# An S5 recurrence beside a gated MLP: output base made with the layer norm, B u over runs of 512 tokens, another order of first loads, another cut of the last tile

## The chip, the cores and the metric

One core of one Trainium2 chip. The metric is device time in microseconds of one launch, as a median of several executions. The span of a profile, from first to last instruction, is about 2 us shorter than the time of the same execution. The kernel before takes 274.86 us (274.7 to 275.23, 4 runs).

## The reference, cut to what matters

```python
xn = _layernorm(x)                      # x: 1 x 2048 x 640
# A: Bu = xn B_bar^T; h = Lam_bar * h + Bu, token by token; y = 2 Re(h C^T) + xn * Dskip
# B: z = gelu(xn w_in); z2 = layernorm(second half of z);
#    g = w_sp z2 + b_sp (mixes over all tokens); (z1 * g) w_out
return x + A(xn) + B(xn)
```

The term `x + xn * Dskip` needs no matmul. It is called *base* below.

## The kernel before

The program is a list of operations with reads, writes and rough durations. A list scheduler inside the kernel puts each engine's operations in an order by a model of their times; TensorE's order is as written. The chip then runs each engine's queue in that order. Token tiles are counted from 0: T0, T1, T2 are the transposes of the first three, x0, x1, x2 the loads of their input. LN is the layer norm. An eviction is the copy of a finished matmul result out of PSUM. The stages are: LN of 16 tiles, the transposes and z2; B u; z1; the mixing over tokens ("spatial products", by a Strassen-like scheme of seven products); the output tiles. VectorE runs the recurrence (`horner`, `scan`) beside them, and ScalarE afterwards adds the state that comes from earlier chunks (`fix`).

The parts that the change touches:

```python
FIRST = "x0 x1 h002 h025 x2 x3 h102 h125 x4 x5"   # loads; h002: half 0 of w_in, k tiles 0 and 1 (h105: half 1, k tiles 0 to 4)
...
def xn_T(i, b=None):                   # transposes of tile i on PE, one copy out of PSUM
    pe(tr, [xn.iv(), ident_m.iv()], [bank(b)], 0.3, "T%d" % i)
    act(lambda e: e.copy(xnTv[:, :, i * 128:(i + 1) * 128], v), ...)
...
def bu(q, jg, half):                   # 4 of every 8 tokens of a half
    rhs = [xnTv[:, k, half * 1024:(half + 1) * 1024].rearrange("p (m j) -> p m j", j=8)[:, :, jg * 4:jg * 4 + 4]
           for k in range(ND)]
...
def out_tile(j, half, b, last=False):
    dma("sp", bsm.ap(D), rows(A_x), ...)                                     # x again
    dve(... tensor_scalar(om, bsm, mean, rstd, subtract, mult) ...)          # xn again
    dve(... tensor_tensor(om, om, dk, mult) ...)                             # * Dskip
    dve(... tensor_tensor(om, om, bsm, add) ...)                             # + x
    ...  # 34 matmuls, each tile as two banks of 320 columns, alternating
    dve(... tensor_tensor(om, ps, om, add) ...)                              # last tile: 320 and 320
```

## Time and profile before

| stretch of the chain | from, us | length, us |
|---|---|---|
| head, to T2, the transposes of the third tile | 0 | 9.67 |
| z2 | 9.67 | 30.02 |
| B u, 200 matmuls | 39.69 | 45.00 |
| z1 | 84.70 | 29.20 |
| spatial products, 448 matmuls | 113.90 | 81.76 |
| output tiles | 195.66 | 73.96 |
| tail, to the end of the span | 269.62 | 3.1 |

The table is read from the chain of work that ended last. Its lines, with start, length and what ran:

```profile
9.67 0.45 PE ps L540 x5
...
39.69 45.00 PE ps L655 x200
...
113.90 81.76 PE ps L963 x448
195.66 2.72 PE ps L1053 x20
...
269.65 0.49 DVE arena L1076
270.14 0.40 DVEq L228
```

From 9.67 to 269.62 us the chain is TensorE alone, each piece starting where the last ends. So what other engines do in between costs nothing, as long as TensorE finds its operands. A B u matmul takes 45.00 / 200 = 225 ns; a spatial product of 432 columns takes 81.76 / 448 = 182.5 ns.

The head in the timeline (start, length, engine, line, operation; in brackets the idle time before it and what ended it):

```profile
5.50 0.98 DVE L526 TENSOR_SCALAR arena<-arena 128x640 bf16<-128x640 bf16 x2 [0.30 <-POOL arena L521]
6.01 0.98 PE L540 MATMUL ps<-arena 128*128 128x128 bf16 x10
6.70 0.49 DVE L515 BATCH_NORM_STATS2 arena<-arena 128x6 f32<-128x320 bf16 x1 [0.22 <-DMA arena<-in_A_x_dram]
7.47 2.00 PE L592 MATMUL ps<-arena 128*128 128x432 bf16 x10 [0.48 <-ACT arena L544]
9.67 0.45 PE L540 MATMUL ps<-arena 128*128 128x128 bf16 x5 [0.20 <-DVE arena L526]
```

L526 gives xn (the normalized x) of tiles 0 and 1, L540 at 6.01 is T0 and T1, L515 at 6.70 is the first statistic of x2, the moment x2 has landed. T2 is at 9.67.

The table of stretches for B u, spatial products and output (length; busy us of PE, PEld, DVE, ACT, POOL with counts; clock; DMA share; GB/s):

```profile
39.69:84.70 45.01, 45.01 (x202) 19.25 (x200) 37.16 (x86) 39.50 (x66) 3.52 (x4) 1.00 0.27 47
113.90:195.66 81.76, 81.76 (x450) 43.86 (x449) 78.11 (x164) 46.03 (x77) 0.00 (x0) 1.00 0.88 185
195.66:269.62 73.96, 73.95 (x544) 52.93 (x542) 50.34 (x115) 30.12 (x50) 0.00 (x0) 1.00 0.37 104
```

VectorE is busy for 50.34 of 73.96 us in the output stage; it has more room there than in the spatial products.

### The profile page before, as it was taken

To read this page: it belongs to the slowest core of one execution; us is meant where nothing else is said; L and a number is where in the kernel's file an instruction comes from. 1 tells how busy PE (TensorE), PEld (TensorE's weight loads), DVE (VectorE), ACT (ScalarE), POOL (GpSimd) and SP (SyncE) were. 2 spreads that over 40 slices of the span, in tenths; PEclk is the share of its full clock that TensorE was granted. 3 is DMA by queue.
4 is the path that set the end of the run, shared out by engine and by line. 5 is a ranking of instruction groups with operands and counts; after the bars stand their busy time and mean duration, and the time that the engine had idled before them with its cause. 6 is when DMAs were issued, how large, how long until landed. Compare 5 with 4: busy or idle time off the path is not lost.

```text
span 272.7 us, 4381 instructions
## 1 busy us (share of the span) xinstructions
PE 267.6 (98%) x1574; PEld 159.3 (58%) x1574; DVE 226.1 (83%) x551; ACT 164.7 (60%) x288; POOL 25.6 (9%) x54
## 2 busy tenths in 40 slices
PE   8999999999999999999999999999999999999995
PEld 3455554444446777755555555555577777777773
DVE  4988947588999999989999996999999995555442
ACT  2899999979976454523223228999999991000000
POOL 4445662200000000000000000000000000000000
PEclk9999999999999999999999999999999999999999
DMA  7999799400002974497996798699454645331201
GB/s 220 284 211 151 174 185 189 66 24 4 0 0 48 199 214 146 150 192 128 209 217 142 168 184 168 123 226 259 165 142 127 164 109 150 93 99 48 92 30 48
DMA packets 84883, 37.82 MB, mean 139 GB/s; under 512 B 70046, under 2 KB 84862, under 8 KB 84862
## 3 DMA queue, kind: packets, MB, share of 16 engines
q1 hardware_dynamic: 84718, 37.47, 61.4%
q8 instruction: 12, 0.20, 0.3%
q10 hardware_dynamic: 144, 0.08, 0.1%
q14 instruction: 9, 0.07, 0.1%
HBM read 12.29 MB, written 8.93 MB: 78 GB/s over the span
## 4 chain that ended last, share of the span: by engine, by line
PE 95%; DMA 1%; DVE 1%; SPq 1%; POOL 0%; issue 0%; DVEq 0%
PE ps L963 30%; PE ps L571 19%; PE ps L655 17%; PE ps L1053 16%; PE ps L1061 11%; PE ps L592 2%; DMA arena<-in_A_x_dram 1%; PE ps L540 1%; SPq L356 1%; DVE arena L515 0%; DVE arena L516 0%; POOL arena L521 0%; DVE arena L1076 0%; DVE arena L526 0%; DVEq L228 0%
## 5 line engine op out<-in xcount | busy, mean ns | idle before, releaser
L963 PE MATMUL ps<-arena 128*128 128x432 bf16 x448 | 81.9, 346 | 0.0
L963 PEld LDWEIGHTS ps<-arena 128*128 128x128 bf16 x448 | 43.8, 98 | 37.9
L571 PE MATMUL ps<-arena 128*128 128x432 bf16 x280 | 52.1, 346 | 0.0
L1053 PE MATMUL ps<-arena 128*128 128x320 bf16 x320 | 46.1, 299 | 0.0
L756 ACT ACTIVATE arena<-arena 128x512 bf16<-128x512 bf16 x70 | 44.0, 714 | 2.1 <-DVE arena L728 2.1
L655 PE MATMUL ps<-arena 128*128 128x512 bf16 x200 | 45.2, 386 | 0.0
L571 PEld LDWEIGHTS ps<-arena 128*128 128x128 bf16 x280 | 34.5, 124 | 15.6
L1053 PEld LDWEIGHTS ps<-arena 128*128 128x128 bf16 x320 | 31.2, 98 | 12.4
L976 ACT ACTIVATE arena<-ps,arena 128x432 f32<-128x432 f32 (+1 forms) x32 | 19.7, 615 | 29.4 <-PE ps L963 23.8
L655 PEld LDWEIGHTS ps<-arena 128*128 128x128 bf16 x200 | 19.2, 96 | 25.8
L1061 PE MATMUL ps<-arena 128*128 128x320 bf16 (+1 forms) x224 | 33.1, 299 | 0.0
L1061 PEld LDWEIGHTS ps<-arena 128*128 128x128 bf16 (+1 forms) x224 | 21.9, 98 | 8.5
L759 DVE TENSOR_TENSOR arena<-arena 128x512 bf16<-128x512 bf16 x70 | 26.2, 419 | 0.3 <-ACT arena L756 0.2
L686 DVE SCALAR_TENSOR_TENSOR arena<-arena 128x512 f32<-128x512 bf16 x35 | 25.8, 749 | 0.0
L662 ACT CAST arena<-ps 128x512 bf16<-128x512 f32 x40 | 21.3, 596 | 5.5 <-PE ps L655 5.4
L1070 DVE TENSOR_TENSOR arena<-ps,arena 128x640 bf16<-128x640 f32 x15 | 12.3, 823 | 12.7 <-PE ps L1061 12.6
L640 ACT ACTIVATE arena<-ps 128x864 bf16<-128x864 f32 x16 | 14.2, 890 | 13.5 <-PE ps L571 12.7
L920 DVE TENSOR_TENSOR arena<-arena 128x1024 bf16<-128x1024 bf16 x32 | 21.3, 686 | 1.2 <-PE ps L963 1.1
L708 DVE TENSOR_TENSOR arena<-arena 128x512 f32<-128x512 f32 (+2 forms) x40 | 21.6, 556 | 0.0
L691 DVE SCALAR_TENSOR_TENSOR arena<-arena 128x256 bf16<-128x256 bf16 (+1 forms) x35 | 16.8, 483 | 0.0
L688 DVE SCALAR_TENSOR_TENSOR arena<-arena 128x256 bf16<-128x256 bf16 (+1 forms) x35 | 16.7, 481 | 0.0
L1037 DVE TENSOR_SCALAR arena<-arena 128x640 bf16<-128x640 bf16 x16 | 7.1, 441 | 7.7 <-DMA out_dram<-arena 7.7
(99 smaller groups left out, 244.0 us busy)
## 6 DMA issues: line engine op xcount, KB each, us to landing
arena<-in_A_x_dram SPq DMA_DIRECT2D x32, 160.0 KB, 2.6
z_scratch<-arena SPq DMA_DIRECT2D x16, 216.0 KB, 2.2
arena<-z_scratch SPq DMA_DIRECT2D x8, 432.0 KB, 5.0
g_scratch<-arena SPq DMA_DIRECT2D x12, 224.0 KB, 2.9
out_dram<-arena SPq DMA_DIRECT2D x15, 160.0 KB, 2.2
arena<-in_B_w_in_dram SPq DMA_DIRECT2D x7, 216.0 KB, 3.6
arena<-in_B_w_out_dram SPq DMA_DIRECT2D x1, 960.0 KB, 6.7
arena<-in_B_w_in_dram SPq DMA_DIRECT2D x2, 324.0 KB, 4.3
```

Source lines behind the costliest of these rows:

```text
L571: r = e.matmul(ps[:, b + h, 0:FG], lhs(k), winv[:, k, hcol * FH + h * FG:hcol * FH + (h + 1) * FG], start=(k == 0), stop=(k == ND - 1))
L655: r = e.matmul(ps[:, b + ri, :], btv[:, ri, k, q * 128:(q + 1) * 128], rhs[k], start=(k == 0), stop=(k == ND - 1))
L662: act(lambda e, ri=ri: e.copy(o[:, ri, :, half, :], ps[:, b + ri, :].rearrange("p (m j) -> p j m", j=4)), [bank(b + ri)], [l_iv(q, jg * 4 ...
L686: dve(lambda e: e.scalar_tensor_tensor(tv, prev, lr, cur, op0=ALU.mult, op1=ALU.add), pr + [l_iv(q, j)] + cr, [t.iv()], cd(512) + PTR, nm ...
L708: tt = lambda o, a, b, op: (lambda e: e.tensor_tensor(o, a, b, op))
L756: act(lambda e, pv=pv, hv=hv, lo=lo, sc=sc: e.activation(pv, hv[:, lo:lo + 2, 1:257], ACT.Identity, scale=sc), [h.iv(), Civ(cn)], [m.iv()] ...
L759: dve(lambda e, m=m, lq=lq: e.tensor_tensor(lq, lq, m.ap(512), ALU.add), li + [m.iv()], li, cd(512, 2), "fix%s%d%d" % (nm, q, j))
L920: dve(lambda e: e.tensor_tensor(o.ap(1024), x.ap(1024), y.ap(1024), op), [x.iv(), y.iv()], [o.iv()], cd(1024, 2), "%s_%d" % (name, j))
L963: r = e.matmul(ps[:, bk, 0:FG], lv_[:, k, :], rv[k], start=(first and k == 0), stop=(k == 7), skip_group_check=True)
L976: act(lambda e: e.activation(o, pb(bk), ACT.Identity, bias=bias), [bank(bk)] + bi, [dst], ca(FG, psum=True, ptr=1), name)
L1053: r = e.matmul(ps[:, b + n, 0:320], hv[:, o:o + 128], cpv[:, ri, q, n * 320:(n + 1) * 320], start=(q == 0 and ri == 0), stop=False, skip_g ...
L1061: r = e.matmul(ps[:, b + n, 0:320], gv[0:kk, k, :], wov[0:kk, k, n * 320:(n + 1) * 320], start=False, stop=(k == 6), skip_group_check=True)
```

## The change

Its intent: compute base once, while x and xn are in SBUF, and spare the output stage its recomputation; read B u's moving operand in a row; let x2 come earlier and release the first z2 sooner; leave less to do after the last matmul. The list scheduler's model is altered too (its constants of latency and DMA rate, how it books transposing DMAs, and a rule for the first 12 us), and a fourth LN tile goes to ScalarE. The core of the diff, cut:

```diff
-    DMA_BW = 230e3
-    DMA_BW_T = 190e3
+    DMA_BW = 280e3
+    DMA_BW_T = 215e3
 ...
-            return g.add("dve", f, r, w, occ, 0.17, name, bias=bias)
+            return g.add("dve", f, r, w, occ, 0.13, name, bias=bias)
 ...                                          # act 0.2 -> 0.15, pool 0.15 -> 0.09
-        FIRST = "x0 x1 h002 h025 x2 x3 h102 h125 x4 x5"
+        FIRST = "x0 x1 h002 x2 h025 x3 h105 x4 x5"
-        ACT_LN = (6, 9, 12)
+        ACT_LN = (6, 8, 10, 12)
 ...
+            if i == 0:                        # T0 in two banks, copied out by two engines
+                act(lambda e: e.copy(xnTv[:, 0:3, 0:128], v[:, 0:3]), ...)
+                dve(lambda e: e.tensor_copy(xnTv[:, 3:5, 0:128], v2[:, 3:5]), ...)
 ...
+        def base(i):
+            dve(... tensor_tensor(m, xn, dk, mult) ...)
+            dve(... tensor_tensor(m, m, x, add) ...)
+            dma("sp", base_d[i * 128:(i + 1) * 128, :], m.ap(D), ...)
 ...
-        def bu(q, jg, half):
+        def bu(q, tq):
-            rhs = [... .rearrange("p (m j) -> p m j", j=8)[:, :, jg * 4:jg * 4 + 4] ...]
+                                     xnTv[:, k, tq * 512:(tq + 1) * 512], ...
 ...
-            dma("sp", bsm.ap(D), rows(A_x), ...)
-            ... xn, * Dskip, + x ...
+            dma("sp", bsm.ap(D), base_d.rearrange("(h r j) d -> h j r d", h=2, j=8)[half, j], ...)
 ...
+            cols = ((0, LASTN), (LASTN, D)) if last else ((0, 320), (320, D))    # LASTN = 480
```

In the last tile the 17 matmuls of the first 480 columns now all come before the 17 of the last 160.

More of the change, by code (lines that the diff above doesn't have):

```diff
@@ L29 @@
 class _Graph:
+    EPS0 = 0.12
+    TEPS = 12.0
     DMA_LAT = 2.0
-    DMA_BW = 230e3
-    DMA_BW_T = 190e3
+    DMA_BW = 280e3
+    DMA_BW_T = 215e3
     def __init__(self):
@@ L129, in schedule @@
                     s0 = min(max(f, o.rdy) for o in lst)
-                    cand = max((o for o in lst if max(f, o.rdy) <= s0 + eps), key=lambda o: o.tail)
+                    cand = max((o for o in lst if max(f, o.rdy) <= s0 + (self.EPS0 if s0 < self.TEPS else eps)), key=lambda o: o.tail)
                     st = max(f, cand.rdy)
@@ L141, in schedule @@
             if op.nbytes:
-                b0 = max(st + op.occ + 0.9, dma_free)
-                bw = self.DMA_BW_T if op.lat > 2.2 else self.DMA_BW
-                dma_free = b0 + op.nbytes / bw
-                op.done = dma_free + op.lat - 0.9
                 if op.lat > 2.2:
-                    free[eng] = max(free[eng], dma_free - 1.0)
+                    dma_free = max(st + 0.3, dma_free) + op.nbytes / self.DMA_BW_T
+                    free[eng] = max(free[eng], dma_free)
+                    op.done = max(st + op.occ, dma_free) + 1.7
+                else:
+                    dma_free = max(st + op.occ + 0.9, dma_free) + op.nbytes / self.DMA_BW
+                    op.done = dma_free + op.lat - 0.9
             else:
@@ L237, in bass_parallel_sum__ssm_conv_s5__mixer_gmlp__prompt_kernel @@
         g_d = nc.dram_tensor("g_scratch", [NT, 128, 896], BF16).ap()
-        stat_d = nc.dram_tensor("stat_scratch", [S, 2], FP32).ap()
+        base_d = nc.dram_tensor("base_scratch", [S, D], BF16).ap()
         class Mem:
@@ L287, in bass_parallel_sum__ssm_conv_s5__mixer_gmlp__prompt_kernel @@
         dk_m = top.sub(1280)
+        e4 = Mem(l_m.lo + 8192, 15 * 1280)
+        x_m += [e4.sub(1280) for _ in range(5)]
+        xn_m += [e4.sub(1280) for _ in range(10)]
+        base_m = [Mem(t_m[(1, 0, 2)[i // 5]].lo + i % 5 * 1280, 1280) for i in range(15)] + [Mem(l_m.lo + 38400, 1280)]
         hs_m = [top.sub(1548) for _ in range(5)]
@@ L335, in dve @@
         def dve(f, r, w, occ, name, bias=0.0):
-            return g.add("dve", f, r, w, occ, 0.17, name, bias=bias)
+            return g.add("dve", f, r, w, occ, 0.13, name, bias=bias)
         def act(f, r, w, occ, name, bias=0.0):
-            return g.add("act", f, r, w, occ, 0.2, name, bias=bias)
+            return g.add("act", f, r, w, occ, 0.15, name, bias=bias)
         def pool(f, r, w, occ, name, bias=0.0):
-            return g.add("pool", f, r, w, occ, 0.15, name, bias=bias)
+            return g.add("pool", f, r, w, occ, 0.09, name, bias=bias)
         def pe(f, r, w, occ, name):
@@ L408, in load_x @@
         def load_x(i, q="sp", bias=0.0):
-            m = x_m[i % 11]
+            m = x_m[i]
             xs[i] = m
@@ L488, in siv @@
             return st_m.iv((i * 16 + a) * 4, (b - a) * 4)
-        ACT_LN = (6, 9, 12)
+        ACT_LN = (6, 8, 10, 12)
         ACT_Z2 = (8, 12)
         NHALF = 4
+        LASTN = 480
         DMA_T = (10, 11, 12, 13, 14, 15)
@@ L501, in ln_x @@
             if i in ACT_LN:
-                sq = xn_m[i % 6]
+                sq = xn_m[i]
                 act(lambda e: e.activation(sq.ap(D), x, ACT.Copy, accum_out=stv[:, i, 0:1]),
@@ L522, in ln_x @@
                  [siv(i, 14, 15), Civ("half")], [ri], 0.5, "rstd%d" % i)
-            xn = xn_m[i % 6]
+            xn = xn_m[i]
             xns[i] = xn
@@ L536, in xn_T @@
             v = ps[:, b, :].bitcast(BF16)[:, 0:D].rearrange("p (u t) -> p u t", u=ND)
+            v2 = ps[:, 6, :].bitcast(BF16)[:, 0:D].rearrange("p (u t) -> p u t", u=ND)
             def tr(e):
                 for u in range(ND):
-                    r = e.transpose(v[:, u, :], xn.ap(D)[:, u * 128:(u + 1) * 128], ident_m.ap(128))
+                    r = e.transpose((v2 if i == 0 and u > 2 else v)[:, u, :], xn.ap(D)[:, u * 128:(u + 1) * 128], ident_m.ap(128))
                 return r
-            pe(tr, [xn.iv(), ident_m.iv()], [bank(b)], 0.3, "T%d" % i)
-            if i % 2 == 0 or i == 1:
+            pe(tr, [xn.iv(), ident_m.iv()], [bank(b)] + ([bank(6)] if i == 0 else []), 0.3, "T%d" % i)
+            if i == 0:
+                act(lambda e: e.copy(xnTv[:, 0:3, 0:128], v[:, 0:3]), [bank(b)],
+                    [xnT_m.iv(k * S * 2, 256) for k in range(3)], ca(384, psum=True), "xnT0a")
+                dve(lambda e: e.tensor_copy(xnTv[:, 3:5, 0:128], v2[:, 3:5]), [bank(6)],
+                    [xnT_m.iv(k * S * 2, 256) for k in (3, 4)], 0.21, "xnT0b")
+            elif i % 2 == 0 or i == 1:
                 act(lambda e: e.copy(xnTv[:, :, i * 128:(i + 1) * 128], v), [bank(b)], xnT_iv(i, i + 1),
@@ L547, in xn_T @@
                 dve(lambda e: e.tensor_copy(xnTv[:, :, i * 128:(i + 1) * 128], v), [bank(b)], xnT_iv(i, i + 1),
-                    cd(D), "xnT%d" % i)
-        def stats_turn():
-            for i in range(NT):
-                if i not in ACT_LN:
-                    pool(lambda e, i=i: e.tensor_copy(mrv[:, i, 0:1], stv[:, i, 12:13]), [siv(i, 12, 13)],
-                         [mr_m.iv(i * 8, 4)], 0.2, "mean%d" % i)
-            dma("sp", stat_d.rearrange("(t p) s -> p t s", p=128), mrv, [mr_m.iv()], [("statd", 0, 1)], 16384, "stst")
-            dma("sp", msv.rearrange("p (h j) s -> p h j s", h=2), stat_d.rearrange("(h r j) s -> r h j s", h=2, j=8),
-                [("statd", 0, 1)], [ms_m.iv()], 16384, "stld")
+                    0.41, "xnT%d" % i)
+        def base(i):
+            m, xn, xm = base_m[i], xns[i], xs[i]
+            dve(lambda e: e.tensor_tensor(m.ap(D), xn.ap(D), dk_m.ap(D), ALU.mult), [xn.iv(), dk_m.iv()], [m.iv()],
+                cd(D, 2), "xd%d" % i)
+            dve(lambda e: e.tensor_tensor(m.ap(D), m.ap(D), xm.ap(D), ALU.add), [m.iv(), xm.iv()], [m.iv()],
+                cd(D, 2), "base%d" % i)
+            dma("sp", base_d[i * 128:(i + 1) * 128, :], m.ap(D), [m.iv()], [("based", i, i + 1)], 128 * D * 2,
+                "bst%d" % i)
         st2v = st2_m.ap(NT * 8, FP32).rearrange("p (s t) -> p s t", t=NT)
@@ L593, in z2_half @@
                                            start=(k == 0), stop=(k == ND - 1)),
-                   xnT_iv(i, i + 1) + [win_m.iv((k * 2 * FH + c) * 2, FG * 2)], [bank(b)], 0.1825, "z2_%d%d.%d" % (i, h, k))
+                   [xnT_m.iv((k * S + i * 128) * 2, 256), win_m.iv((k * 2 * FH + c) * 2, FG * 2)], [bank(b)], 0.1825, "z2_%d%d.%d" % (i, h, k))
             z = z2v[:, i, h * FG:(h + 1) * FG]
@@ L644, in z1_tile @@
             dma("sp", z1_d[n], m.ap(FH), [m.iv()], [("z1d", n, n + 1)], 128 * FH * 2, "z1st%d" % n, sem=sem)
-        def bu(q, jg, half):
+        def bu(q, tq):
             b = pair()
-            rhs = [xnTv[:, k, half * 1024:(half + 1) * 1024].rearrange("p (m j) -> p m j", j=8)[:, :, jg * 4:jg * 4 + 4]
-                   for k in range(ND)]
             def mm(e):
@@ L654, in mm @@
                     for ri in range(2):
-                        r = e.matmul(ps[:, b + ri, :], btv[:, ri, k, q * 128:(q + 1) * 128], rhs[k],
-                                     start=(k == 0), stop=(k == ND - 1))
-                return r
-            pe(mm, xnT_iv(half * 8, half * 8 + 8) + [bt_m.iv()], [bank(b), bank(b + 1)], 2.16,
-               "bu%d%d%d" % (q, jg, half))
-            o = l_m.ap(2048, BF16, (q * 8 + jg * 4) * 1024).rearrange("p (j r h m) -> p r j h m", j=4, r=2, h=2)
+                        r = e.matmul(ps[:, b + ri, :], btv[:, ri, k, q * 128:(q + 1) * 128],
+                                     xnTv[:, k, tq * 512:(tq + 1) * 512], start=(k == 0), stop=(k == ND - 1))
+                return r
+            pe(mm, xnT_iv(tq * 4, tq * 4 + 4) + [bt_m.iv()], [bank(b), bank(b + 1)], 2.16, "bu%d%d" % (q, tq))
+            o = l_m.ap(4096, BF16, q * 8192).rearrange("p (j r t m) -> p r t j m", j=8, r=2, t=4)
             for ri in range(2):
-                act(lambda e, ri=ri: e.copy(o[:, ri, :, half, :], ps[:, b + ri, :].rearrange("p (m j) -> p j m", j=4)),
-                    [bank(b + ri)], [l_iv(q, jg * 4 + j, ri, half) for j in range(4)], ca(512, psum=True),
-                    "u%d%d%d%d" % (q, jg, half, ri))
+                act(lambda e, ri=ri: e.copy(o[:, ri, tq], ps[:, b + ri, :].rearrange("p (m j) -> p j m", j=8)),
+                    [bank(b + ri)], [l_m.iv((q * 8 + j) * 1024 + ri * 512 + tq * 128, 128) for j in range(8)],
+                    ca(512, psum=True), "u%d%d%d" % (q, tq, ri))
         nh = [0]
@@ L1034, in out_tile, with mmh @@
             rows = lambda a: a[0].rearrange("(h r j) d -> h j r d", h=2, j=8)[half, j]
-            dma("sp", bsm.ap(D), rows(A_x), [], [bsm.iv()], 128 * D * 2, "bld%d%d" % (j, half), sem=sem)
-            nt = half * 8 + j
-            dve(lambda e: e.tensor_scalar(om.ap(D), bsm.ap(D), msv[:, nt, 0:1], msv[:, nt, 1:2], op0=ALU.subtract,
-                                          op1=ALU.mult),
-                [bsm.iv(), ms_m.iv()], [om.iv()], cd(D, 4) + 2 * PTR, "xp%d%d" % (j, half))
-            dve(lambda e: e.tensor_tensor(om.ap(D), om.ap(D), dk_m.ap(D), ALU.mult), [om.iv(), dk_m.iv()],
-                [om.iv()], cd(D, 2), "xd%d%d" % (j, half))
-            dve(lambda e: e.tensor_tensor(om.ap(D), om.ap(D), bsm.ap(D), ALU.add), [om.iv(), bsm.iv()],
-                [om.iv()], cd(D, 2), "base%d%d" % (j, half))
+            dma("sp", bsm.ap(D), base_d.rearrange("(h r j) d -> h j r d", h=2, j=8)[half, j], [("based", 0, 16)],
+                [bsm.iv()], 128 * D * 2, "bld%d%d" % (j, half), sem=sem)
             gt = gt_of[(j, half)]
             gv = gt.ap(896).rearrange("p (k t) -> p k t", k=7)
-            def mmh(e):
+            cols = ((0, LASTN), (LASTN, D)) if last else ((0, 320), (320, D))
+            def mmh(e, ns=(0, 1)):
                 for q in range(5):
@@ L1051, in mmh, with mmg @@
                         o = ri * 256 + half * 128
-                        for n in range(2):
-                            r = e.matmul(ps[:, b + n, 0:320], hv[:, o:o + 128], cpv[:, ri, q, n * 320:(n + 1) * 320],
+                        for n in ns:
+                            lo, hi = cols[n]
+                            r = e.matmul(ps[:, b + n, 0:hi - lo], hv[:, o:o + 128], cpv[:, ri, q, lo:hi],
                                          start=(q == 0 and ri == 0), stop=False, skip_group_check=True)
                 return r
-            def mmg(e):
+            def mmg(e, ns=(0, 1)):
                 for k in range(7):
                     kk = 128 if k < 6 else 96
-                    for n in range(2):
-                        r = e.matmul(ps[:, b + n, 0:320], gv[0:kk, k, :], wov[0:kk, k, n * 320:(n + 1) * 320],
+                    for n in ns:
+                        lo, hi = cols[n]
+                        r = e.matmul(ps[:, b + n, 0:hi - lo], gv[0:kk, k, :], wov[0:kk, k, lo:hi],
                                      start=False, stop=(k == 6), skip_group_check=True)
                 return r
-            pe(mmh, [l_iv(q, j) for q in range(5)] + [cp_m.iv()], [bank(b), bank(b + 1)], 20 * 0.136,
-               "oh%d%d" % (j, half))
-            pe(mmg, [gt.iv(), wo_m.iv()], [bank(b), bank(b + 1)], 14 * 0.136, "og%d%d" % (j, half))
+            rh = [l_iv(q, j) for q in range(5)] + [cp_m.iv()]
+            if last:
+                for n in range(2):
+                    w = (cols[n][1] - cols[n][0]) / 2350 + 0.003
+                    pe(lambda e, n=n: mmh(e, (n,)), rh, [bank(b + n)], 10 * w, "oh%d%d%d" % (j, half, n))
+                    pe(lambda e, n=n: mmg(e, (n,)), [gt.iv(), wo_m.iv()], [bank(b + n)], 7 * w, "og%d%d%d" % (j, half, n))
+            else:
+                pe(mmh, rh, [bank(b), bank(b + 1)], 20 * 0.136, "oh%d%d" % (j, half))
+                pe(mmg, [gt.iv(), wo_m.iv()], [bank(b), bank(b + 1)], 14 * 0.136, "og%d%d" % (j, half))
             dst = rows(out)
@@ L1069, in out_tile @@
             if not last:
-                dve(lambda e: e.tensor_tensor(v(om), ps[:, b:b + 2, 0:320], v(om), ALU.add),
-                    [bank(b), bank(b + 1), om.iv()], [om.iv()], cd(D), "o%d%d" % (j, half))
+                dve(lambda e: e.tensor_tensor(v(om), ps[:, b:b + 2, 0:320], v(bsm), ALU.add),
+                    [bank(b), bank(b + 1), bsm.iv()], [om.iv()], cd(D), "o%d%d" % (j, half))
                 dma("sp", dst, om.ap(D), [om.iv()], [("out", j * 2 + half, j * 2 + half + 1)], 128 * D * 2,
@@ L1074, in out_tile @@
             else:
-                for n, q in ((0, "sp"), (1, "act")):
-                    dve(lambda e, n=n: e.tensor_tensor(v(om)[:, n], ps[:, b + n, 0:320], v(om)[:, n], ALU.add),
-                        [bank(b + n), om.iv(n * 640, 640)], [om.iv(n * 640, 640)], cd(320), "o%d%d%d" % (j, half, n))
-                    dma(q, dst[:, n * 320:(n + 1) * 320], v(om)[:, n], [om.iv(n * 640, 640)],
-                        [("out", 32 + n, 33 + n)], 64 * D * 2, "st%d%d%d" % (j, half, n))
+                for n, (q, lo, hi) in enumerate((("act", 0, LASTN), ("sp", LASTN, D))):
+                    dve(lambda e, n=n, lo=lo, hi=hi: e.tensor_tensor(om.ap(D)[:, lo:hi], ps[:, b + n, 0:hi - lo],
+                                                                    bsm.ap(D)[:, lo:hi], ALU.add),
+                        [bank(b + n), bsm.iv(lo * 2, (hi - lo) * 2)], [om.iv(lo * 2, (hi - lo) * 2)], cd(hi - lo),
+                        "o%d%d%d" % (j, half, n))
+                    dma(q, dst[:, lo:hi], om.ap(D)[:, lo:hi], [om.iv(lo * 2, (hi - lo) * 2)],
+                        [("out", 32 + n, 33 + n)], 256 * (hi - lo), "st%d%d%d" % (j, half, n))
         for i in range(5):
@@ L1118, in bass_parallel_sum__ssm_conv_s5__mixer_gmlp__prompt_kernel @@
                 kappa()
+            if i >= 8:
+                base(i - 8)
             if i % 4 == 3:
                 z2_norm(i - 3, i + 1)
-        stats_turn()
+        for i in range(8, NT):
+            base(i)
         for k in range(ND):
@@ L1125, in bass_parallel_sum__ssm_conv_s5__mixer_gmlp__prompt_kernel @@
         for q in range(5):
-            for jg in range(2):
-                for half in range(2):
-                    bu(q, jg, half)
+            for tq in range(4):
+                bu(q, tq)
             if q < 4:
```

## The prediction

> **What bounds the kernel now.** TensorE. The chain of waits is 95% PE: from 9.67 to 269.62 us matmuls follow without a gap (the list of waits has no later PE wait), at full granted clock. Only three places can give time: the head (before 9.67), the rate of the matmuls, the tail (269.6 to 272.7). Work taken from other engines in the middle is worth nothing unless it starves PE.
>
> **Matmul rate (B u).** The chain gives 200 B u matmuls of 512 columns in 45.00 us: 225 ns each. Others: 432 columns in 182.5 ns, 320 in 136, 128 in 56, all N/2.4 GHz + 2.6 ns. The Trainium skill, "TensorE: Matmul & The Clock Gate" (Part 1), says the same (215.7 ns at N = 512). B u is 9 ns over that, and it alone has a moving operand that takes 4 elements (8 bytes), then skips 4. The skill's "SBUF" page (16-byte cachelines, two hits enough) would expect no penalty; I lay it to the stride. Read in a row, 200 x 9 ns = 1.8 us are saved. The eviction reads PSUM at stride 8 instead of 4 (mean 596 ns, two per 2.16 us); it should stay under 1.08 us, so PE never waits.
>
> **Head.** In the timeline T0 starts at 6.01 us, as the 11 warm-up matmuls end, so earlier LN gains nothing. ACT's copy of the transposed tile releases z2 at 7.47; split into 384 columns on ACT and 256 on DVE it should come 0.2 us sooner. PE idles 0.2 us before T2 at 9.67, as x2 landed only at 6.68, fifth in the queue. As fourth it lands about 1.2 us earlier, so T2 follows at about 9.1. The one load h105 should land by 9 us, just ahead of its use. Gain 0.5 us (0.1 to 0.7).
>
> **Tail.** After the last matmul DVE does two adds of 320 columns, to 270.54 us, then the last store is issued and takes 1.6 us. With 480 and 160 columns the first add runs under the second part's 17 matmuls of 69 ns; only one add of 160 columns (about 0.3 us) follows PE. Gain 0.6 us. PE's sum is unchanged.
>
> **Moved, not gained.** Two DVE operations a tile (0.48 and 0.49 us; 15.5 us in all) go from the output stage, where DVE is half idle, to LN and B u; 7.1 us of recomputed xn and the stats round trip go. By the table of stretches DVE has 12 us free between 10 and 70 us; ACT is full up to 50 us and gets one more LN tile (1.9 us). The recurrence may end some us later; but ACT starts its fix work at about 163 us and the output matmuls at 195.7, so there is slack. The danger is a short PE stall: u of q = 1 overwrites x and xn at about 50 us and waits for base; base ahead of an xn on DVE, or its stores ahead of transposes in the SP queue, can delay a z2 tile. I allow 0.3 us.
>
> **Prediction.** 274.95 - 1.8 - 0.5 - 0.6 + 0.3 = about 272.3 us; 8 in 10 between 271.3 and 273.8. Faster by over 2%: 0.02; within 2%: 0.96; slower: 0.02.
>
> **What would show it.** B u at 43.2 us in the chain (216 ns each); T2 at about 9.1 us; one 160-column add after the last matmul; no PE wait over 0.3 us after 10 us; the output stage still 4.6 us a tile, DVE less busy there.
>
> **What would make it wrong.** B u stays at 225 ns (not the stride): about 274. A PE wait in z2 or early B u for base, DVE or ACT: 1 to 4 us lost. h105 or h025 landing late.

## The result, and the profile after

The changed kernel takes 272.72 us (272.08 to 273.14, 4 runs). The ratio is 0.9918, with a 95% interval of 0.9896 to 0.9941: 2.2 us faster. A ratio is the mean time of one kernel's runs over that of the other's in the same rounds, so it is not quite the ratio of the medians. The total came 0.4 us above the forecast; of its parts, two did not come as forecast.

The chain of the changed kernel, same columns:

```profile
9.66 0.43 PE ps L550 x5
...
39.64 43.17 PE ps L669 x200
...
112.00 30.67 PE ps L976 x168
142.68 0.58 DVE arena L996
...
168.90 0.52 ACT arena L989
...
169.46 24.99 PE ps L976 x136
194.46 2.72 PE ps L1062 x20
...
268.45 0.33 DVE arena L1092
```

Stage by stage, after minus before: T2 9.66 against 9.67; B u 43.17 against 45.00 (-1.83 us); z1 equal; spatial products 194.46 - 112.00 = 82.46 against 81.76 (+0.70); output 73.97 against 73.96; from the last matmul to the end of the span 270.8 - 268.43 = 2.4 against 3.1 (-0.7). With 0.05 us at the start of B u this makes the whole difference of the spans, 272.7 - 270.8 = 1.9 us. The rest of the 2.2 us lies outside the traced span. Time minus span is 2.04 us on average in the 31 runs of the kernel before that were made with the experiments, and 1.98 to 2.13 in the five timed kernels without the base move; it is 1.80 to 1.83 in all seven sets of runs with it. So moving base also takes some 0.2 us off outside the span; why is not known.

New is the break in the chain at 168.90: TensorE waited for an eviction of ScalarE (L989). Before that eviction the chain leaves TensorE at 142.68 and runs along VectorE until 166.9; in the second profile of this kernel it runs almost only along VectorE from 36 us on. VectorE is busy for 129.4 of the 130 us from 36 to 166 in both, so what ScalarE waits for comes only when a VectorE with next to no idle time gets to it. The head, which was to give 0.5 us, gave nothing. Its timeline:

```profile
5.04 0.49 DVE L523 BATCH_NORM_STATS2 arena<-arena 128x6 f32<-128x320 bf16 x1 [0.16 <-DMA arena<-in_A_x_dram]
6.00 0.45 PE L550 MATMUL ps<-arena 128*128 128x128 bf16 x5 [0.81 <-DVE arena L534]
6.96 0.20 DVE L525 BATCH_NORM_AGGREGATE arena<-arena 128x2 f32<-128x12 f32 x1
7.92 0.50 DVE L523 BATCH_NORM_STATS2 arena<-arena 128x6 f32<-128x320 bf16 x1 [0.76 <-DMA arena<-in_A_x_dram]
8.33 0.14 DVE L527 TENSOR_SCALAR arena<-arena 128x1 f32<-128x1 f32 x1
9.64 0.45 PE L550 MATMUL ps<-arena 128*128 128x128 bf16 x5 [0.41 <-DVE arena L527]
```

x2 landed at 5.04 us, 1.66 us earlier than before. Its statistics were joined at 6.96. The next small step for x2 (L527, called lne2 below) could have followed at once, but in VectorE's queue the statistics of x3 stand ahead of it, and x3 landed only at 7.92. The Trainium skill, "TensorE: Matmul & The Clock Gate" (the table at its head), says that the queues of ScalarE and VectorE are strictly first in, first out; this trace agrees for VectorE, with 0.76 us in which it stood idle while lne2 was ready.

The stretches after, same columns as before:

```profile
39.64:82.81 43.17, 43.17 (x201) 19.69 (x200) 42.61 (x111) 40.43 (x70) 5.15 (x5) 1.00 0.50 120
112.00:194.46 82.46, 81.94 (x451) 43.70 (x449) 82.29 (x172) 44.67 (x74) 0.00 (x0) 1.00 0.89 185
194.46:268.43 73.97, 73.95 (x544) 52.50 (x542) 33.31 (x69) 31.60 (x53) 0.00 (x0) 1.00 0.37 101
```

The base move did what it says: VectorE is busy 33.31 instead of 50.34 us in the output stage. The output stage is as long as it was. In B u VectorE now has 0.6 us free instead of 7.9, and in the spatial products 0.2 instead of 3.7.

### The profile page after: what moved, and what is told of

The parts are those of the page before. It is cut to its first block, busy times and chain, and to the rows that moved or that the text cites. A ratio compares the mean times of both kernels' runs of the same rounds, so it can differ in the third digit from the quotient of the medians.

```text
span 270.8 us, 4388 instructions
## 1 busy us (share of the span) xinstructions
PE 264.9 (98%) x1574; PEld 158.6 (59%) x1574; DVE 219.4 (81%) x536; ACT 165.6 (61%) x292; POOL 24.2 (9%) x41
## 4 chain that ended last, share of the span: by engine, by line
PE 86%; DVE 9%; DMA 2%; issue 1%; ACT 1%; SPq 1%; DVEq 0%; ACTq 0%
PE ps L976 21%; PE ps L586 19%; PE ps L1062 16%; PE ps L669 16%; PE ps L1071 11%; DVE arena L721 2%; PE ps L607 2%; DMA arena<-in_A_x_dram 2%; DVE arena L933 2%; DVE arena L996 1%; PE ps L550 1%; SPq L363 1%; DVE arena L730 1%; DVE arena L1017 1%; DVE arena L701 0%
## 5 line engine op out<-in xcount | busy, mean ns | idle before, releaser
L1062 PE MATMUL ps<-arena 128*128 128x320 bf16 (+2 forms) x320 | 46.3, 299 | 0.0
L769 ACT ACTIVATE arena<-arena 128x512 bf16<-128x512 bf16 x70 | 44.1, 720 | 1.1 <-DVE arena L741 1.1
L669 PE MATMUL ps<-arena 128*128 128x512 bf16 x200 | 43.3, 379 | 0.0
L989 ACT ACTIVATE arena<-ps,arena 128x432 f32<-128x432 f32 (+1 forms) x32 | 19.8, 618 | 32.5 <-PE ps L976 29.6
L1071 PE MATMUL ps<-arena 128*128 128x320 bf16 (+4 forms) x224 | 33.2, 299 | 0.0
L772 DVE TENSOR_TENSOR arena<-arena 128x512 bf16<-128x512 bf16 x70 | 27.5, 422 | 4.3 <-ACT arena L769 3.7
L721 DVE TENSOR_TENSOR arena<-arena 128x512 f32<-128x512 f32 (+2 forms) x40 | 21.0, 546 | 0.0
L933 DVE TENSOR_TENSOR arena<-arena 128x1024 bf16<-128x1024 bf16 x32 | 20.7, 678 | 0.0
L701 DVE SCALAR_TENSOR_TENSOR arena<-arena 128x256 bf16<-128x256 bf16 (+1 forms) x35 | 16.5, 473 | 0.0
L704 DVE SCALAR_TENSOR_TENSOR arena<-arena 128x256 bf16<-128x256 bf16 (+1 forms) x35 | 16.4, 474 | 0.0
L600 ACT ACTIVATE arena<-arena 128x864 bf16<-128x864 bf16 x12 | 11.2, 937 | 0.0
```

Of the source, the lines that this page charges most:

```text
L669: r = e.matmul(ps[:, b + ri, :], btv[:, ri, k, q * 128:(q + 1) * 128], xnTv[:, k, tq * 512:(tq + 1) * 512], start=(k == 0), stop=(k == ND ...
L721: tt = lambda o, a, b, op: (lambda e: e.tensor_tensor(o, a, b, op))
L769: act(lambda e, pv=pv, hv=hv, lo=lo, sc=sc: e.activation(pv, hv[:, lo:lo + 2, 1:257], ACT.Identity, scale=sc), [h.iv(), Civ(cn)], [m.iv()] ...
L772: dve(lambda e, m=m, lq=lq: e.tensor_tensor(lq, lq, m.ap(512), ALU.add), li + [m.iv()], li, cd(512, 2), "fix%s%d%d" % (nm, q, j))
L933: dve(lambda e: e.tensor_tensor(o.ap(1024), x.ap(1024), y.ap(1024), op), [x.iv(), y.iv()], [o.iv()], cd(1024, 2), "%s_%d" % (name, j))
L989: act(lambda e: e.activation(o, pb(bk), ACT.Identity, bias=bias), [bank(bk)] + bi, [dst], ca(FG, psum=True, ptr=1), name)
```

## The experiments

Twelve further kernels were run, one of them the changed kernel again. All passed the comparison with the reference. So did the stride probe, whose columns are wrong: the comparison is no strict check of B u.

### Each part alone

Four kernels put one part each on the kernel before, in the same rounds on one chip.

**B u alone.**

```diff
-        def bu(q, jg, half):
+        def bu(q, tq):                       # as in the change
```

> Only B u reads runs of 512 tokens in a row; everything else as before. Stride theory: the 200 B u matmuls take 43.2 us in the chain instead of 45.0 (216 ns each). Time: if the PE wait of 0.5 to 0.7 us in the spatial products of the changed kernel comes from the base work moved onto VectorE (theory A), there is none here and the time is 1.8 us under before, about 273.0. If it comes from PE running 1.8 us ahead of a VectorE that is not faster (theory B), the spatial products take about 82.4 us here too and the time is about 273.7.

Measured: 273.21 us, ratio 0.9932 (0.9919 to 0.9946), so 1.9 us faster. In the chain B u takes 43.17 us and the spatial products 81.76, with no PE wait there. Theory B falls.

**Base alone.**

```diff
+        def base(i):                         # with the LN, as in the change; 16 x and 16 xn buffers
-        stats_turn()
-            dma("sp", bsm.ap(D), rows(A_x), ...)     # and three DVE operations
+            dma("sp", bsm.ap(D), base_d..., ...)
```

> Only the base work is moved to LN and kept in DRAM; B u, head and tail as before. Theory A (base fills VectorE, so the recurrence ends late and ScalarE, in order, holds an eviction back): a PE wait of 0.5 us or more among the spatial products, which take about 82.4 us instead of 81.8, and a time of 0.5 to 0.8 us over before. Theory B: no PE wait, time as before within 0.2 us.

Measured: 274.46 us, ratio 0.9984 (0.9971 to 0.9996). The spatial products take 81.76 us with no PE wait. Theory A falls. The gain of 0.4 us is barely clear of noise. About half of it lies outside the span, as above (1.83 us on average instead of 2.04). The other half may be chance: in the profile T2 came at 9.49 instead of 9.67, as x2 happened to land at 6.5 us.

**The tail alone.**

```diff
+        LASTN = 480
+            cols = ((0, LASTN), (LASTN, D)) if last else ((0, 320), (320, D))
```

> Only the last tile is cut as 480 and 160 columns. From the last matmul to the end of the span about 2.4 us instead of 3.1: 0.7 us faster than before, about 274.2. If the gain of the tail belongs to the base work that is no longer there, 0.2 us or less.

Measured: 274.25 us, ratio 0.9976 (0.9963 to 0.9990), 0.7 us faster. One addition of 0.33 us follows the last matmul, in place of two. The gain is the cut's own. The edit also makes the last store smaller, 160 columns instead of 320. In the whole change the last addition ends 0.57 us sooner after the last matmul than before; the other 0.14 us of the 0.71 lie after it, where the store is, and were not tested apart.

**The head alone.**

```diff
-        FIRST = "x0 x1 h002 h025 x2 x3 h102 h125 x4 x5"
+        FIRST = "x0 x1 h002 x2 h025 x3 h105 x4 x5"
+                ... T0 in two banks, copied out by ScalarE and VectorE
```

> Only the order of the first loads and the cut of the first transposed tile over two engines. The changed kernel starts T2 at 9.66 us, before at 9.67, because VectorE's queue has bn_stats of x3 (landing at 7.9 us) ahead of the step that releases x2's rstd. Here, with the old constants of the kernel's own list scheduler, the queue may be another: if lne2 stands ahead, T2 starts at 9.1 to 9.3 us and the time is 0.4 us under before; if not, T2 stays at 9.6 to 9.7 and the time is the same within 0.2 us.

Measured: 275.01 us, ratio 1.0001 (0.9988 to 1.0013). T2 did come earlier, at 9.38 us, but then the chain went through the one load of the second half of the weights, and through ScalarE:

```profile
3.63 6.22 DMA arena<-in_B_w_in_dram
...
9.90 1.10 PE ps L599 x5
...
11.02 0.63 ACT arena L604 x2
...
25.07 14.77 PE ps L578 x80
```

h105 landed at 9.85 us, not by 9. Up to 25 us the chain is ScalarE's, whose copies of transposed tiles and gelus are back to back there. B u starts at 39.85, no earlier than before (39.69). T0 itself came at 6.52 instead of 6.01, because xn waited behind x2's statistics (more of this below). So four things stood between the head and its 0.5 us: VectorE's queue order ahead of T2 and ahead of T0, the landing of the weights, and a full ScalarE.

### What the stride costs

```diff
+                    if n == 0:
+                        return x[:, 0:512]
+                    ...
+                    if n == 6:
+                        return x[:, 0:2048].rearrange("p (m j) -> p m j", j=8)[:, :, 0:2]
+                    ...                       # ten ways, 20 matmuls each, a source line each
```

> Wrong results on purpose: B u with ten ways of drawing its 512 columns from a row of x transposed, 20 matmuls each, on the kernel before. In order: 512 in a row; in a row from column 4; 8 of 16; 4 of 8 (as before); 16 of 32; 2 of 4; 2 of 8; 1 of 2; 1 of 4; 4 of 16. If nothing in the moving operand matters, all are 216 ns, or 225. If each break of a run costs: 216, 216, 221, 225, 218, 234, 234, 253, 253, 225 ns. If each 16-byte line beyond 64 costs: 216, 216, 216, 225, 216, 225, 244, 225, 244, 225 ns.

The chain gives each group of 20, in the order named there (left out are the second and third, 4.32 us each as well):

```profile
39.98 4.32 PE ps L680 x20
...
52.93 4.50 PE ps L686 x20
57.43 4.32 PE ps L688 x20
61.75 4.50 PE ps L690 x20
66.25 9.02 PE ps L692 x20
75.27 4.50 PE ps L694 x20
79.77 9.02 PE ps L696 x20
88.79 4.58 PE ps L698 x20
```

Divided by 20: 216 ns in a row, also from column 4, and for 8 of 16 or 16 of 32; 225 ns for 4 of 8, 2 of 4 and 1 of 2; 451 ns for 2 of 8 and 1 of 4; 229 ns for 4 of 16. The number of breaks doesn't matter (64 breaks cost nothing; 1 of 2 has more breaks than 4 of 8 and costs the same). What matters is how many of a 16-byte line's 8 bf16 elements are used: 8, then 4, then 2. The class of 2 per line shows how it works: 512 columns with 2 per line touch 256 lines, and 451 / 256 = 1.76 ns; with 4 per line they touch 128, and 225 / 128 = 1.76 ns too. So in these runs a line takes at least 1.76 ns. The columns themselves take (216 - 182.5) / 80 = 0.42 ns each, so four take 1.68 ns: 4 per line is just short of full speed, and that shortfall was B u's 9 ns. Neither of the first two theories fits. Of the third the classes were right, but the cost of the 2-per-line class was far off (244 expected): the time is the larger of two rates, not a sum. One thing the rule does not explain: 4 of 16 touches 128 lines as 4 of 8 does, but takes 229 ns, 4 ns more.

### The PE wait in the spatial products

**All four parts, old constants of the scheduler.**

```diff
-    DMA_BW = 280e3                           # and the rest of the model back to that of before
+    DMA_BW = 230e3
-        ACT_LN = (6, 8, 10, 12)
+        ACT_LN = (6, 9, 12)
```

> All four parts of the change (B u, base, head, tail) with the old constants of the kernel's own list scheduler and the old choice of three LN tiles on ScalarE. Neither B u alone nor base alone showed a PE wait in the spatial products (81.76 us each), the whole change did (82.46). Theory AB (the two together: PE 1.8 us earlier and VectorE filled by base): the spatial products take 82.2 us or more here too, about 272.7. Theory C (the new constants set an order of the queues in which ScalarE holds an eviction behind a wait for VectorE): 81.8 us and no PE wait, about 272.1.

Measured: 271.97 us (271.8 to 272.56), ratio 0.9899 (0.9886 to 0.9912); spatial products 81.76 us, no PE wait. Theory AB falls, as a cause that is enough by itself. In this kernel ScalarE's queue has the eviction p5 ahead of the first `fix`, and two pieces of `fix` before the next eviction (166.29, 166.70 and 167.94 us in its trace). The ratios of the four single parts add to 0.9932 + 0.9976 + 0.9984 + 1.0001 - 3 = 0.9893, which this kernel reaches within its interval and the changed kernel's ratio of 0.9918 doesn't.

**The change without base.**

```diff
-        for i in range(8, NT):
-            base(i)
+        stats_turn()                         # and the output stage as before
```

> The whole change without the base move: B u, head, tail and the new constants; xn and base recomputed in the output stage as before. If base is needed for the wait (theory A or AB): spatial products 81.8 us, no PE wait there, about 272.1, so 0.6 us faster than the whole change. Theory C: 82.2 us or more, about 272.7.

Measured: 274.09 us (272.48 to 274.25, 6 runs), ratio 0.9958 (0.9939 to 0.9978): 1.4 us slower than even the worse expectation. The spatial products take 81.96 us, with 0.2 us of loss left, so a little of the wait is there without base. TensorE reached them 1.9 us later here than in the changed kernel (113.93 against 112.00), so this trace can't tell how large the wait would be at the same start, and the test decides neither way. The rest of the surprise is in the head, told below.

**Another order of VectorE's queue in the head.**

```diff
-    EPS0 = 0.12
+    EPS0 = 0.16
```

> The whole change with one number of the list scheduler altered (0.12 to 0.16 for the first 12 us), which puts the step that releases x2's rstd ahead of bn_stats of x3 in VectorE's queue. If VectorE's queue order is what kept T2 at 9.66 us and the only thing: T2 at about 9.2 us and B u starts 0.4 us earlier (39.2 instead of 39.64). If the one load h105 is next (it landed 9.85 us in head_only): T2 earlier, but the matmuls after it still start at 9.85 to 9.95 us, and B u starts at 39.5 to 39.8 as before.

Measured: 272.1 us, ratio 0.9902 (0.9889 to 0.9915). The head gained nothing: T2 at 9.85, B u from 40.05. The step for x2 did run ahead of x3's statistics, but x2 landed at 6.10 us and T0 came only at 6.99, so T2 stood behind other matmuls; what the queue order alone is worth was not measured. But the spatial products take 81.76 us, without a PE wait. All the new constants are in this kernel, so theory C in its plain form (these constants bring the wait) falls too. The order of the queues did change, and TensorE came 0.41 us later; a later TensorE alone doesn't spare the wait, since the second profile of the changed kernel (below) starts its spatial products at 112.32 us, 0.09 before this one, and has it.

ScalarE's queue around the wait, in the changed kernel:

```profile
166.32 0.72 ACT L769 ACTIVATE arena<-arena 128x512 bf16<-128x512 bf16 x1 [1.10 <-DVE arena L741]
166.96 0.81 ACT L891 ACTIVATE arena<-arena 128x640 bf16<-128x640 bf16 x1
167.67 0.50 ACT L987 COPY arena<-ps 128x432 f32<-128x432 f32 x1
168.07 0.83 ACT L893 ACTIVATE arena<-arena 128x640 bf16<-128x640 bf16 x1
168.80 0.60 ACT L989 ACTIVATE arena<-ps,arena 128x432 f32<-128x432 f32 x1
169.46 2.73 PE L976 MATMUL ps<-arena 128*128 128x432 bf16 x14 [0.52 <-ACT arena L989]
```

and in this experiment:

```profile
165.95 0.72 ACT L769 ACTIVATE arena<-arena 128x512 bf16<-128x512 bf16 x1 [0.32 <-DVE arena L741]
166.58 0.50 ACT L987 COPY arena<-ps 128x432 f32<-128x432 f32 x1
166.98 0.83 ACT L891 ACTIVATE arena<-arena 128x640 bf16<-128x640 bf16 x1
167.71 0.82 ACT L893 ACTIVATE arena<-arena 128x640 bf16<-128x640 bf16 x1
168.43 0.60 ACT L989 ACTIVATE arena<-ps,arena 128x432 f32<-128x432 f32 x1
```

The same three pieces of filling work (one L769, the first of `fix`; L891; L893) stand ahead of the same eviction L989. In the changed kernel L769 held the queue for 1.10 us, waiting for the end of VectorE's scan (L741), and the eviction came late; here it held it for 0.32 us, and the eviction came in time. L769 started 0.37 us earlier here, and TensorE's spatial products 0.41 us later. In the kernel before, the same wait was longer, 2.1 us, but stood in a wide gap between evictions and cost nothing:

```profile
164.81 0.72 ACT L756 ACTIVATE arena<-arena 128x512 bf16<-128x512 bf16 x1 [2.07 <-DVE arena L728]
```

**Three instructions moved in ScalarE's queue.**

```diff
+        by["P00"].start = by["p5_5"].start + 0.001      # L769 behind L987
+        by["cy00"].start = by["u2_5"].start + 0.001     # L891, L893 behind L989
+        by["cy01"].start = by["u2_5"].start + 0.002
         lists = g.waits()
```

> The whole change with three instructions moved in ScalarE's queue alone: the first scaling of the fix behind the eviction p5 of the sixth spatial product group, two scalings of C behind its eviction u2. If the PE wait comes from these standing ahead of the evictions while VectorE's scan is late: spatial products 81.76 us, no PE wait there, and 0.5 to 0.7 us under the whole change in the same rounds (about 272.0). If not: 82.3 to 82.5 us and the same time.

Measured: 272.88 us (271.91 to 274.72, 6 runs). The changed kernel, run again on the same chip:

> The whole change again, for comparison on one chip: 272.6 to 272.8 us, spatial products 82.3 to 82.5 us with the PE wait at about 169 us. If the wait is there only in some executions, the times spread over 1 us as in its first four runs (272.08 to 273.14), against 0.3 us for the reordered one.

Measured: 272.58 us (272.2 to 274.24, 6 runs), ratio 0.9927; the PE wait is there (169.57 us), and the spatial products take 82.24 us. The reordered kernel takes 82.48 us there and is not faster, with or without the executions at clock 0.994 (without: medians of 272.66 and 272.42): the test failed. In its trace L769 no longer waits and L989 comes in time, at 169.55, but then five filling pieces (4 of 0.72 us, one of 0.61) stand ahead of the *next* eviction, at 173.56, and TensorE waits at 174.22. I had moved the work from one filled gap to another. So it shows that filling work ahead of an eviction can hold TensorE here with no wait for VectorE at all; it doesn't show that taking the scan's wait away is enough. The profiled execution also began its spatial products 2.0 us later than the changed kernel's, for a reason in the head that comes next, so VectorE had that much more time in it anyway.

### The head that depends on when x2 lands

The executions of the changed kernel spread more than those of before (274.25 to 275.26 on this chip), and one of six took 274.24 us, with a mean clock of 0.994. The reordered kernel has the same head, and two of its six did so: 274.65 and 274.72 us, clock 0.994; one of them is the profiled one:

```profile
6.10 0.49 DVE L523 BATCH_NORM_STATS2 arena<-arena 128x6 f32<-128x320 bf16 x1 [0.98 <-DMA arena<-in_A_x_dram]
6.57 0.44 DVE L534 TENSOR_SCALAR arena<-arena 128x640 bf16<-128x640 bf16 x1
7.06 0.45 PE L550 MATMUL ps<-arena 128*128 128x128 bf16 x5 [1.67 <-DVE arena L534]
...
8.47 3.37 PE L607 MATMUL ps<-arena 128*128 128x432 bf16 x10
```

In the changed head, the first statistic of x2 (L523) stands in VectorE's queue *ahead of* xn of tile 0 (L534). x2 landed at 6.10 us here (5.04 in the first profile of the changed kernel, 5.95 in its second), so T0 came at 7.06 instead of 6.00. TensorE stood idle for 1.67 us after its warm-up, and the clock fell: ten matmuls took 3.37 us instead of 2.0. B u starts at 41.67 us. The profile of the kernel without base shows the same (T0 at 7.08, B u from 41.56 instead of 39.64, clock 0.994); that accounts for the surprise in the profiled run, and the two others of its six with clock 0.994 fit it; one of 274.00 us at full mean clock is not explained. A late T0 is the rule, not the exception: of the eight profiles with x2 fourth, only the first of the changed kernel has it at 6.00, the other seven at 6.52 to 7.08. The clock fell in two of them. With the load order of before, xn of tile 0 stands ahead of x2's statistics, and T0 comes at 5.98 to 6.05 us in the profiles of the kernel before, of B u, base and tail alone, and of B u, tail and base together, though x2's statistics start anywhere between 6.5 and 7.3 us.

### Versions that might beat both

**B u, tail and base, with the head and the constants of before.**

```diff
-        FIRST = "x0 x1 h002 x2 h025 x3 h105 x4 x5"
+        FIRST = "x0 x1 h002 h025 x2 x3 h102 h125 x4 x5"      # T0 in one bank, old constants
```

> B u, tail and base without the head part and with the old constants. If the head part is worth nothing or costs some tenths (x2 fourth puts its bn_stats ahead of the first xn in VectorE's queue): 271.6 to 272.0 us, T0 at 6.0 us, B u starting at 39.5 to 39.9 us. If the head part is worth the predicted 0.5 us: 272.3 us or more.

Measured: 272.22 us (271.73 to 272.65), ratio 0.9902 (0.9887 to 0.9918). T0 at 5.98; x2 landed late this time (7.33), so B u starts at 40.32, yet there is no PE wait later. By ratio it stands with the kernel with old constants (0.9899): no gain of the head part shows.

**B u and tail with a head of my own.**

```diff
+        FIRST = "x0 x1 h002 x2 h025 h102 h125 x3 x4 x5"
-        xn_T(3, 1)
         z2_half(1, 1, 7)
         z2_half(2, 0, 4)
+        xn_T(3, 1)
```

> B u and tail on the kernel before, and another head: x2 fourth, the second half of the weights as two loads ahead of x3, the split first tile, and T3 moved behind two more z2 halves, so that neither x3 nor the second half of the weights is awaited. If the head was held by when the weights land: T2 at about 9.1 to 9.3 us, the matmuls after it right behind, B u starting at 39.2 to 39.4 us; no PE wait later; about 271.9, under the whole change by 0.8. If the head cannot be shortened by order (the bytes set it): T2 or the matmuls after it at 9.6 us or later, about 272.3.

Measured: 273.13 us, ratio 0.9933 (0.9920 to 0.9945): a miss by 1.2 us. T0 came at 6.85 (x2's statistics again stand ahead of xn), T2 at 9.71, and from 9.91 to 25.82 us the chain is ScalarE's; B u starts at 40.64. My order cost a microsecond.

Best of all by median is the four parts with the old constants, 271.97 us against 272.72 (and 272.58) of the changed kernel; their intervals overlap (0.9886 to 0.9912 and 0.9896 to 0.9941), so that it is faster than the changed kernel is likely and not shown.

## Why the prediction was right or wrong

- **What bounds the kernel: right.** All differences within the span lie in where TensorE starts, runs slower or waits. Freeing VectorE of 17 us in the output stage changed that stage by 0.01 us.
- **B u, 1.8 us: right in size and mechanism.** 43.17 us in the chain (43.2 forecast), alone as in the whole. The probe shows the stride to be the cause.
- **Eviction of B u at stride 8: right.** Its median is 594 ns against 592, and TensorE never waits for it.
- **Tail, 0.6 us: right.** 0.7 us, also alone.
- **Head, 0.5 us: wrong; it gave nothing.** The step that failed is "As fourth it lands about 1.2 us earlier, so T2 follows at about 9.1". x2 landed 1.66 us earlier in the profiled run, but VectorE's queue put x3's statistics ahead of x2's next step. "The one load h105 should land by 9 us" failed as well: 9.85 in the head alone. "T0 starts at 6.01 us, as the 11 warm-up matmuls end, so earlier LN gains nothing" took a coincidence of one profile for the rule: in those of B u, base and tail alone the warm-up ends at 5.4 to 5.7 us, and TensorE then waits 0.39 to 0.65 us for xn. So T0 hangs on LN, and the new order can make it *later*, which it did in seven of eight profiles.
- **The allowance of 0.3 us for a PE stall: right that one comes, wrong place and too small.** I looked for it in z2 and early B u. It is 0.70 us in the spatial products, at an eviction (0.48 in the second profile). "The recurrence may end some us later; but ... there is slack" was true of the work that needs the recurrence and missed that ScalarE's queue, in order, mixes that work with evictions TensorE needs.
- **Why the sum held all the same:** -1.83 - 0.05 - 0.71 + 0.70 = -1.9 us of span. Head and stall were forecast at -0.5 and +0.3, and came as 0 and +0.7. These misses don't cancel; they add to about 0.8 us. The total is only 0.4 us above the forecast because the tail gave a tenth more and because some 0.2 us fell away outside the span, which nobody forecast. That part is luck.

Open: why just this order of queues brings the wait. Neither B u nor base brings it alone, nor do all four parts with the old constants; the new constants with one head number altered don't either. A full VectorE is not enough: in that last kernel it is busy for 129.7 of the 130 us from 36 to 166, and there is no wait. I take it for an accident of the list order on ScalarE and VectorE, but the one test that was to show this failed.

## What to carry to other kernels

Where one engine's chain is gapless, cost a change by three things only: where that chain starts, how fast its instructions run, and what follows its last one; moved work earned nothing inside the traced span here (some 0.2 us outside it) and can still fill a queue that feeds the chain. An earlier load is worth something only when the in-order queue that consumes it has nothing that waits for a later load ahead of the next step, and a statistic placed ahead of critical work turns a variable landing time into a variable start. Read a matmul's nanoseconds per column for each shape: the one that stands out (225 ns where the others' line gives 216) was the largest gain in this change.

## What the Trainium skill lacked or had wrong

- "SBUF — State Buffer", Specifications (TRN2), says that at least two hits per 16-byte line are needed for full bandwidth, and that each cross to a new line pays a penalty; it gives no size for either. For a bf16 moving operand of 512 columns two or four hits are not enough: 2 of 8 elements per line take 451 ns, 4 of 8 take 225, all 8 take 216 (1.76 ns per line at least). With all 8, the 64 lines show no penalty above the N/2.4 + 2.5 ns of the next point.
- "TensorE: Matmul & The Clock Gate", Part 1, has N/2.4 + 2.5 ns per matmul, 215.7 ns at N = 512. The runs agree (43.17 us / 200 = 216 ns), for operands that use whole lines; the page doesn't name the moving operand's stride as a condition.
- The same section gives the cold state "after ≥1 idle window (~3.4µs)". Here a pause of 1.67 us after a warm-up from 1.31 to about 5.4 us, and five transposes with another 0.45 us of pause behind it, were enough to lose the clock (ten 432-column matmuls in 3.37 us instead of 2.0); in the run with the altered head number a pause of 1.56 us, with ten transposes together after it, was not. How much idle time within a window drops the clock is on no page that I used.
